# Expert outputs of an RWKV-5 and mixture-of-experts kernel: transposed by VectorE into pieces of 96 values, and one prefix product placed earlier

## The chip, the cores and the metric

The kernel runs on one core of a Trainium2 chip. The metric is the device time of one execution in microseconds. Before the change it is 455.46 us, the median of 9 runs that lie between 454.89 and 457.84 us. All profiles are of one execution on that core; times in them count from the first instruction of the span. Engines are TensorE (PE; its weight loads are PEld), VectorE (DVE), ScalarE (ACT), GpSimd (POOL) and SyncE (SP, which only issues DMAs here).

## The reference

Two blocks follow each other, everything in FP32.

The first is a recurrence over time (RWKV-5): 4 batches, 8 heads, 768 steps, a head of 48 values. Its outputs, taken as 3072 rows (tokens) of 384 values, enter the second block, a mixture of experts in two levels: 4 groups of 4 experts. Each token goes to one expert, and its result is scaled by two softmax weights:

```python
g_idx = np.argmax(x @ w_group, axis=1)
# within the chosen group g:
e_idx = np.argmax(xg @ w_expert[g], axis=1)
# for the tokens of expert (g, e):
h = np.maximum(xg[mask_e] @ w1[g, e], 0.0)     # 384 -> 1024
ye = h @ w2[g, e]                              # 1024 -> 384
out[tok_idx] = combined[:, None] * ye          # combined: product of the two gates
```

So each token is computed by one of 16 experts of 384 x 1024 and 1024 x 384 weights (3 MB together), and its row goes back to the place of the token.

## The kernel before

**First stage** (to about 155 us). 24 tiles of 128 tokens go through the recurrence in matrix form, in a loop of 29 steps in which each tile is at another point of its way (`turn`, `scores`, `values`, `back`, `rows_T`, `row_logits`). The order of the instructions of all engines is that of the program text here. `route` works out the choice of tokens in groups of two or four tiles, in five parts that the loop places at steps of its own: `choice` (arg-max, one-hot, exponential), `before` (L395: two products that count, for every token, how many tokens of its expert come ahead of it: the prefix product), `gate` (softmax weights), `place` (L417: the row number in the expert's region) and `rows` (L423: an indirect DMA by GpSimd that writes 128 rows of 384 values and two extra ones, the token's number and its gate, into `x_sorted`). `choice`, `before` and `gate` work in the PSUM bank `rb`, and the products of `before` go into a part of that bank, `pre`.

**Second stage.** `ITEMS` (L469) is a list of 17 pieces of work. Item 0 is the first 128 tokens of the fullest expert after four sixths of the tokens, which begins inside the first stage; item 1 is the rest of that expert, up to 256; items 2 to 16 are the other experts, in the order of their sizes. Each has a fixed number of slots (`SLOTS`, L20: 256, 240, 233, ... 178, 173). Tokens that don't fit would be done by a part at the end that these inputs don't need.

For an item:

- `load_rows` (L488, SP queue) reads the item's rows of `x_sorted` in blocks of 32 tokens, and the two extra values (`key`) with 128 tokens on partitions.
- `columns` (L508, VectorE) turns each 32 x 32 block, so that `xe` has the model dimension on partitions and tokens along the free dimension; then makes `ids` (token numbers) and `gates`, one token to a partition.
- `up` (L523, PE) computes two of eight blocks of 128 hidden values: the weights `w1` are the stationary operand (lhsT) and the tokens the moving one. ScalarE applies the ReLU into `hT`.
- `down` (L538, PE) computes one of three blocks of 128 output values, with 128 contiguous columns of `w2` as lhsT, over eight steps. ScalarE copies PSUM to `yo`, which has output values on partitions and tokens along the free dimension.
- `rows_out` (L571) calls `turn_out` (L555): TensorE transposes `yo` in blocks of 128 x 128 into PSUM (`pb`, L565), VectorE scales each row by its gate into `yt` (L567), and GpSimd scatters 128 rows of 384 values into `out` by an indirect DMA (L577). For 233 slots that is six transposes, two scalings and two DMAs.

Of item i, `rows_out` stands between `up(i + 1, 2)` and `up(i + 1, 4)`; for the last item a part of it stands inside its own last `down`. Weights have two places, the tiles `w1`/`w2` and the space of `kall`/`rall` of the first stage; the weights of expert e + 2 are issued on SP's queue when those of e have been read (L444, L449). In this stage only PE's order is written out; that of the other engines is made by the scheduler.

**The passage.** The last group of two tiles is routed while item 0 is computed. `before`, `gate`, `place` and the two `rows` of this group stand after `up(0, 4)` (L817 to L819). Item 1 can be loaded only when all rows are scattered: L821 follows on SP's queue and waits for the landing. Between stand `up(0, 6)`, `down(0, 0)` to `down(0, 2)` and `rows_out(0)` on PE.

Of the kernel before, what the change touches and what calls it, by code (L numbers as in the profile page):

```python
# [15 lines left out]
P = 128  # L16
# [18 lines left out]
def kernel(  # L35
# [312 lines left out]

    def route(pool, rb, xt, T, sums, number, group):

# [20 lines left out]
        place_f = part(1, "p (i a) -> p i a")  # L371
        pre = part(GE, "p (i e) -> p i e")
        mx, kx = tl([P, T, NA], "mx"), tl([P, T, NA], "kx")
# [108 lines left out]
    def room(i):  # L482
        return P if i == 0 else CAP

    def padded(n):
        return -(-n // BL) * BL

    def load_rows(i, expert, queue):  # L488
# [8 lines left out]
        n = room(i)  # L497
        xg, key = xgs[i] = tl([P, n // BL, KO, BL], "xg"), tl([P, n // P, ROW_EXTRA], "key")
        a, w, rows = ITEMS[i][1], padded(width(i)), regions[bass.ds(expert, 1)]
        for q in range(P // BL):  # L500
# [3 lines left out]
            )  # L504
        n = P * len(parts(i))
        queue.dma_start(out=key[:, 0 : n // P], in_=rows[:, a : a + n, DM:XW].rearrange("a (j p) w -> p (a j) w", p=P))

    def columns(i):  # L508
        xg, key = xgs.pop(i)
        w = padded(width(i))  # L510
        xe = xes[i] = item_tile(i, [P, KO, room(i)], "xe")
        for ko in range(KO):
            nc.vector.transpose(xe[:, ko, 0:w].rearrange("p (b t) -> p b t", t=BL), xg[:, 0 : w // BL, ko, :])  # L513
        ids = item_tile(i, [P, 2], "ids", U32, bufs=4)
        gates = item_tile(i, [P, 2], "gates", bufs=4)
        for j, n in enumerate(parts(i)):
            nc.vector.tensor_scalar(
                out=ids[0:n, j : j + 1], in0=key[0:n, j, ROW_ID : ROW_ID + 1], scalar1=float(N), scalar2=None, op0=OP.add
            )
            nc.vector.tensor_copy(gates[0:n, j : j + 1], key[0:n, j, ROW_GATE : ROW_GATE + 1])  # L520
        keys_of[i] = ids, gates

    def up(i, f):  # L523

# [4 lines left out]
        ph = bank([P, 2, w], "ph")  # L529
        for q in range(2):  # L530
            for ko in range(KO):
                nc.tensor.matmul(  # L532
                    ph[:, q, :], lhsT=w1[:, ko, P * (f + q) : P * (f + q + 1)], rhs=xe[:, ko, 0:w],
                    start=(ko == 0), stop=(ko == KO - 1), skip_group_check=True,
                )
        nc.scalar.activation(hTs[i][:, f : f + 2, 0:w], ph, AF.Relu)  # L536

    def down(i, d, beside=None):  # L538

        w = width(i)  # L540
        if d == 0:
            yo[i] = item_tile(i, [P, KO, room(i)], "yo")
        w2, hT = weights[ITEMS[i][0]][1], hTs[i]
        po = bank([P, w], "po")
        for fo in range(FO):
            if fo == FO // 2 and beside is not None:
                beside()
            nc.tensor.matmul(  # L548
                po, lhsT=w2[:, fo, P * d : P * (d + 1)], rhs=hT[:, fo, 0:w], start=(fo == 0), stop=(fo == FO - 1)
            )  # L550
# [4 lines left out]
    def turn_out(i, d0, d1):  # L555
# [6 lines left out]
        for j, n in enumerate(parts(i)):  # L562
            pb, yt = out_rows[i][j]
            for d in range(d0, d1):
                nc.tensor.transpose(pb[0:n, P * d : P * (d + 1)], yo[i][:, d, P * j : P * j + n], ident)  # L565
            cols = slice(P * d0, P * d1)
            nc.vector.tensor_scalar(  # L567
                out=yt[0:n, cols], in0=pb[0:n, cols], scalar1=gates[0:n, j : j + 1], scalar2=None, op0=OP.mult
            )

    def rows_out(i, d0=0):  # L571
# [138 lines left out]
    def routing(n):  # L710
# [5 lines left out]
            rpool, lgs.pop(n), xts[c][:, b0 : b + 1, :], T, cum[:, first : n + 2, :], tok[:, c, b0 : b + 1],  # L716
            "rows to places",
        )
# [97 lines left out]
    up(0, 2)  # L816
    up(0, 4)  # L817
    for _, part in todo.pop(NT + LAST):
        part()  # L819
# [24 lines left out]
    down(0, 2)  # L844
    rows_out(0)
    load_rows(2, second, nc.sync)
# [5 lines left out]
    with ExitStack() as moe:  # L852
        pools[1] = moe.enter_context(tc.tile_pool(name="moe", bufs=2, reuse_waits="tile"))
        with tc.manual_schedule(engines={mybir.EngineType.PE}):
            columns(1)
            for i in range(1, len(ITEMS)):
                up(i, 0)
                up(i, 2)
                if i > 1:
                    rows_out(i - 1)  # L860
                up(i, 4)
# [243 lines left out]
```

## Time and profile before

| | |
|---|---|
| median of 9 runs | 455.46 us (454.89 to 457.84) |
| the profiled execution | 454.51 us, span 452.7 us |
| TensorE busy | 430.9 us (95%) |
| its weight loads | 417.0 us (92%) |
| VectorE, ScalarE, GpSimd busy | 157.2, 138.9, 130.2 us |
| first product of the experts (L532), two groups | 72.9 and 68.4 us |
| second product (L548), two groups | 69.6 and 67.2 us |
| transposes of the outputs (L565) | 96, 13.7 us |
| row scalings (L567) | 34, 18.6 us |
| scatters into `out` (L577) | 32, 34.2 us |
| mean granted TensorE clock | 0.990 |
| DMA | 86.64 MB, 191 GB/s over the span |

Busy time of an engine is the time in which at least one of its instructions runs. TensorE's instructions overlap: a matmul of 196 columns lasts 0.33 us and starts 0.166 us after the one before. What one costs in a full stretch is therefore read from the starts in the timeline, and not from its length. In a group's line, "x" is the count, then come the busy time, the mean length in ns, and after the second bar the idle time of the engine ahead of these instructions with what ended it. The queue of SyncE is written SPq. An FP32 matmul appears as two records, a transpose as one.

### The profile page before, as it was taken

The numbers are of one execution on the slowest core, as the hardware profiler recorded it, in microseconds if no ns is written. First come the engines' busy times: TensorE is split into PE (matmuls) and PEld (weight loads), VectorE is DVE, ScalarE is ACT, GpSimd is POOL, SyncE is SP. The second block draws the span as 40 slices with busy tenths as digits, with TensorE's granted clock in tenths as the row PEclk, the third lists the DMA queues.
The fourth block names the chain that finished last, engine by engine and source line by source line (L and its number), as shares of the span: only waits on it lengthen the run. The fifth ranks groups of instructions, "written<-read, shape, count | busy, mean of one in ns | idle before, by whom it ended". The sixth has DMA issues, their size and how long they took to land. (4 is left out here: it accounts for less than half of the span.)

```text
span 452.7 us, 9343 instructions
## 1 busy us (share of the span) xinstructions
PE 430.9 (95%) x3553; PEld 417.0 (92%) x3553; DVE 157.2 (35%) x499; ACT 138.9 (31%) x418; POOL 130.2 (29%) x135
## 2 busy tenths in 40 slices
PE   7899999999999897999999999999999999999991
PEld 6699999899998797999999999999999999999991
DVE  6575777867785762011010110110110110111011
ACT  2885565456555321111111211211211121111110
POOL 7855536666653140001010210110210110221011
PEclk9999999999999989999999999999999999999997
DMA  9999999970117636999998887997997999999000
GB/s 171 240 244 223 251 268 228 186 141 36 38 37 177 206 109 157 266 266 197 278 260 203 207 236 163 256 244 168 252 251 172 264 243 213 233 246 245 30 25 27
DMA packets 126592, 86.64 MB, mean 191 GB/s; under 512 B 99532, under 2 KB 116084, under 8 KB 126540
## 3 DMA queue, kind: packets, MB, share of 16 engines
q1 hardware_dynamic: 115532, 69.19, 67.1%
q0 software_dynamic: 4624, 9.48, 6.4%
q10 hardware_dynamic: 6384, 7.31, 4.7%
q8 instruction: 29, 0.48, 0.5%
q14 instruction: 23, 0.19, 0.1%
HBM read 70.16 MB, written 16.12 MB: 191 GB/s over the span
## 5 line engine op out<-in xcount | busy, mean ns | idle before, releaser
L577 POOL DMA_INDIRECT out_dram<-yt,ids x32 | 34.2, 1068 | 242.7 <-DVE yt L567 238.1
L567 DVE TENSOR_SCALAR yt<-pb,gates 128x384 f32<-128x384 f32 (+18 forms) x34 | 18.6, 587 | 231.0 <-PE pb L565 231.0
L532 PE MATMUL ph<-xe,w 128*128 128x128 f32 (+7 forms) x432 | 72.9, 327 | 3.5 <-DVE xe L513 2.7
L532 PEld LDWEIGHTS ph<-xe,w 128*128 128x128 f32 x432 | 69.6, 196 | 4.2 <-issue 2.9
L548 PE MATMUL po<-hT,w 128*128 128x128 f32 (+7 forms) x432 | 69.6, 321 | 0.0
L536 ACT ACTIVATE hT<-ph 128x256 f32<-128x256 f32 (+15 forms) x68 | 33.6, 494 | 114.5 <-PE ph L532 99.0
L532 PE MATMUL ph<-xe,kall 128*128 128x240 f32 (+7 forms) x384 | 68.4, 335 | 0.2 <-DMA kall<-in_moe_w_dram 0.2
L548 PEld LDWEIGHTS po<-hT,w 128*128 128x128 f32 x432 | 68.0, 190 | 0.3
L548 PE MATMUL po<-hT,rall 128*128 128x240 f32 (+7 forms) x384 | 67.2, 334 | 0.0
L548 PEld LDWEIGHTS po<-hT,rall 128*128 128x128 f32 x384 | 65.3, 190 | 0.6
L532 PEld LDWEIGHTS ph<-xe,kall 128*128 128x128 f32 x384 | 64.9, 190 | 0.9 <-PE po L548 0.4
L551 ACT COPY yo<-po 128x128 f32<-128x128 f32 (+15 forms) x51 | 16.4, 321 | 115.1 <-PE po L548 115.1
L607 ACT ACTIVATE dv<-vt,du 128x48 f32<-128x48 f32 x192 | 45.9, 324 | 1.5 <-DVE du L601 1.5
L637 DVE TENSOR_TENSOR am<-pa,later 128x512 f32<-128x512 f32 x48 | 30.9, 686 | 6.8 <-PE pa L632 6.6
L425 POOL DMA_INDIRECT x_sorted<-xt,place_i x24 | 23.8, 990 | 27.0 <-DVE xe L513 13.8
L632 PE MATMUL pa<-rT,kT 48*128 48x128 f32 x384 | 28.7, 285 | 1.2 <-issue 0.7
L596 POOL TENSOR_TENSOR dg<-rall,kall 128x768 f32<-128x768 f32 x12 | 21.9, 1827 | 25.5 <-DVE du L601 25.5
L591 POOL TENSOR_TENSOR kh<-kall,T 128x768 f32<-128x768 f32 (+1 forms) x12 | 21.6, 1802 | 18.7 <-DMA kall<-in_k_dram 17.1
L632 PEld LDWEIGHTS pa<-rT,kT 48*128 48x128 f32 x384 | 23.9, 187 | 3.0 <-issue 1.1
L654 PE MATMUL py<-am,vt 128*64 128x128 f32 x384 | 26.5, 279 | 0.0
L622 ACT COPY kT<-pk 128x512 f32<-128x512 f32 x24 | 14.0, 584 | 34.0 <-PE pk L618 26.8
L654 PEld LDWEIGHTS py<-am,vt 128*64 128x64 f32 x384 | 20.7, 136 | 3.2 <-issue 0.5
(128 smaller groups left out, 439.6 us busy)
## 6 DMA issues: line engine op xcount, KB each, us to landing
w<-in_moe_w_dram SPq DMA_DIRECT2D x32, 384.0 KB
w<-in_moe_w_dram SPq DMA_DIRECT2D x8, 1536.0 KB
kall<-in_moe_w_dram SPq DMA_DIRECT2D x32, 384.0 KB
rall<-in_moe_w_dram SPq DMA_DIRECT2D x8, 1536.0 KB
x_sorted<-nothing ACTq DMA_DIRECT2D x4, 1544.0 KB
rall<-in_r_dram SPq DMA_DIRECT2D x12, 384.0 KB
vt<-in_v_dram SPq DMA_DIRECT2D x12, 384.0 KB
kall<-in_k_dram SPq DMA_DIRECT2D x10, 384.0 KB
```

The costliest lines, as they stand in the source:

```text
L425: ins = nc.gpsimd.indirect_dma_start(out=xs_dram, out_offset=bass.IndirectOffsetOnAxis(ap=place_i[:, i : i + 1], axis=0), in_=xt[:, i, :], ...
L532: nc.tensor.matmul(ph[:, q, :], lhsT=w1[:, ko, P * (f + q) : P * (f + q + 1)], rhs=xe[:, ko, 0:w], start=(ko == 0), stop=(ko == KO - 1), s ...
L536: nc.scalar.activation(hTs[i][:, f : f + 2, 0:w], ph, AF.Relu)
L548: nc.tensor.matmul(po, lhsT=w2[:, fo, P * d : P * (d + 1)], rhs=hT[:, fo, 0:w], start=(fo == 0), stop=(fo == FO - 1))
L567: nc.vector.tensor_scalar(out=yt[0:n, cols], in0=pb[0:n, cols], scalar1=gates[0:n, j : j + 1], scalar2=None, op0=OP.mult)
L577: ins = nc.gpsimd.indirect_dma_start(out=out, out_offset=bass.IndirectOffsetOnAxis(ap=ids[0:n, j : j + 1], axis=0), in_=yt[0:n], in_offset ...
L591: engine.tensor_mul(khs[g % (RING - 1)][:, a0:a1, :, 0:D], kts[g % RING][:, a0:a1], spread(T2[m], 1, a1 - a0))
L596: nc.gpsimd.tensor_mul(dg, rts[g % RING][:, :, :, 0:D], kts[g % RING])
L607: nc.scalar.mul(dv[:, h, :], vts[g % (RING + 1)][:, a, h, 0:D], dvs[g][:, a, h : h + 1])
L632: nc.tensor.matmul(pa[e][:, hc, :], lhsT=kT[rows, hc, :], rhs=rT[rows, hc, :], start=True, stop=True, skip_group_check=True,)
L637: nc.vector.tensor_mul(am[:, e], pa[e], spread(later, 1, HP))
L654: nc.tensor.matmul(py[DP * e : DP * (e + 1), hc, :], lhsT=vt[:, a, 2 * hc + e, :], rhs=am[:, e, hc, :], start=(c == 0), stop=True, skip_gr ...
```

## The change

1. For all items but the last, `rows_out` is replaced by `pieces_out`. VectorE turns `yo` in blocks of 32 x 32 (three instructions, one for each third of the output values), writing with a step of three values; one product scales by the gates; GpSimd scatters. A token's row is now spread over four partitions, one of each quarter, with 96 values in each, and so goes out as four pieces: one indirect DMA writes 128 pieces of 96 values, for 32 tokens.
2. For these pieces to be contiguous in the output, block d of `down` computes the output values d, d + 3, d + 6, ... instead of 128 neighbouring ones. The lhsT of `down` is therefore a view of `w2` with a step of three values, for all items, the last one too. The last item's `turn_out` undoes it by writing `yt` with that step.
3. `key` is loaded with 32 tokens on partitions; `ids` and `gates` hold each number four times, once for every quarter of the partitions, as numbers of pieces (eight small operations instead of four).
4. Where an item's slots are no multiple of 32, the rest of `yo` is filled with zeros.
5. `pieces_out(0)` stands in the second stage, after `columns(1)` in the text; the others stand where `rows_out` stood.
6. The last group's `before` runs inside `up(0, 4)`, between its two halves, and its `pre` has a PSUM bank of its own.

```diff
-    def route(pool, rb, xt, T, sums, number, group):
+    def route(pool, rb, xt, T, sums, number, group, apart=False):
...
-        pre = part(GE, "p (i e) -> p i e")
+        pre = bank([P, T, GE], "pre") if apart else part(GE, "p (i e) -> p i e")
...
-        xg, key = xgs[i] = tl([P, n // BL, KO, BL], "xg"), tl([P, n // P, ROW_EXTRA], "key")
+        xg, key = xgs[i] = tl([P, n // BL, KO, BL], "xg"), tl([P, n // BL, ROW_EXTRA], "key")
...
-        n = P * len(parts(i))
-        queue.dma_start(out=key[:, 0 : n // P], in_=rows[:, a : a + n, DM:XW].rearrange("a (j p) w -> p (a j) w", p=P))
+        p = P if is_last(i) else BL
+        n = -(-w // p) * p
+        queue.dma_start(out=key[0:p, 0 : n // p], in_=rows[:, a : a + n, DM:XW].rearrange("a (j p) w -> p (a j) w", p=p))
...
+            for q in range(P // BL):
+                part, b = slice(BL * q, BL * (q + 1)), w // BL
+                nc.vector.tensor_scalar(
+                    out=ids[part, 0:b], in0=key[0:BL, 0:b, ROW_ID], scalar1=float(P // BL),
+                    scalar2=float(N * (P // BL) + q), op0=OP.mult, op1=OP.add,
+                )
+                nc.vector.tensor_copy(gates[part, 0:b], key[0:BL, 0:b, ROW_GATE])
...
-    def up(i, f):
+    def up(i, f, beside=None):
...
         for q in range(2):
+            if q == 1 and beside is not None:
+                beside()
...
             yo[i] = item_tile(i, [P, KO, room(i)], "yo")
+            if w < padded(w):
+                nc.vector.memset(yo[i][:, :, w : padded(w)], 0.0)
...
-                po, lhsT=w2[:, fo, P * d : P * (d + 1)], rhs=hT[:, fo, 0:w], start=(fo == 0), stop=(fo == FO - 1)
+                po, lhsT=w2[:, fo].rearrange("p (c k) -> p k c", k=KO)[:, d], rhs=hT[:, fo, 0:w], start=(fo == 0), stop=(fo == FO - 1)
...
-                out=yt[0:n, cols], in0=pb[0:n, cols], scalar1=gates[0:n, j : j + 1], scalar2=None, op0=OP.mult
-            )
+                out=yt[0:n].rearrange("p (c k) -> p k c", k=KO)[:, d0:d1],
+                in0=pb[0:n, cols].rearrange("p (k c) -> p k c", c=P),
+                scalar1=gates[0:n, j : j + 1], scalar2=None, op0=OP.mult,
+            )
+
+    def pieces_out(i):
+
+        y, (ids, gates) = yo.pop(i), keys_of.pop(i)
+        w = padded(width(i))
+        b = w // BL
+        yr = item_tile(i, [P, room(i) // BL, BL, KO], "yr")
+        for d in range(KO):
+            nc.vector.transpose(yr[:, 0:b, :, d], y[:, d, 0:w].rearrange("p (b t) -> p b t", t=BL))
+        yp = item_tile(i, [P, room(i) // BL, KO * BL], "yp")
+        nc.vector.tensor_mul(
+            yp[:, 0:b], yr[:, 0:b].rearrange("p b d k -> p b (d k)"), spread(gates[:, 0:b], 2, KO * BL)
+        )
+        out_pieces = out.rearrange("n (q d) -> (n q) d", d=KO * BL)
+        for j in range(b):
+            ins = nc.gpsimd.indirect_dma_start(
+                out=out_pieces, out_offset=bass.IndirectOffsetOnAxis(ap=ids[:, j : j + 1], axis=0), in_=yp[:, j],
+                in_offset=None, bounds_check=N * (P // BL) - 1, oob_is_err=False,
+            )
...
-            "rows to places",
+            "rows to places", n == NT - 1,
...
-    up(0, 4)
-    for _, part in todo.pop(NT + LAST):
+    placing = [part for _, part in todo.pop(NT + LAST)]
+    up(0, 4, placing[0])
+    for part in placing[1:]:
         part()
...
-    rows_out(0)
     load_rows(2, second, nc.sync)
...
             columns(1)
+            pieces_out(0)
...
                 if i > 1:
-                    rows_out(i - 1)
+                    pieces_out(i - 1)
```

## The prediction

> **What bounds the kernel now.** I read the page's busy table first, then the groups by line, then the timeline of one middle item, then that of the passage into the expert stage, and last the DMA share in 2 us windows.
>
> The page's busy table and one of its groups (busy us, mean ns of one | idle before):
>
> ```profile
> PE 430.9 (95%) x3553; PEld 417.0 (92%) x3553; DVE 157.2 (35%) x499; ACT 138.9 (31%) x418; POOL 130.2 (29%) x135
> ...
> L577 POOL DMA_INDIRECT out_dram<-yt,ids x32 | 34.2, 1068 | 242.7 <-DVE yt L567 238.1
> ```
>
> TensorE is full, the others are a third full; what leaves PE shortens the run, if nothing else becomes late. Three groups by line:
>
> ```profile
> L565 PE MATMUL pb<-ident,yo 128*128 128x128 f32 (+15 forms) x96 | 13.7, 274 | 0.5 <-ACT yo L551 0.4
> L565 PEld LDWEIGHTS pb<-ident,yo 128*128 128x128 f32 (+15 forms) x96 | 11.3, 134 | 1.5 <-ACT yo L551 1.0
> L654 PEld LDWEIGHTS py<-am,vt 128*64 128x64 f32 x384 | 20.7, 136 | 3.2 <-issue 0.5
> ```
>
> L565 is what the change takes away: 96 transposes. Of L654 I use the length of a 64-column weight load. Next, the timeline inside the item with 196 tokens (start us, length us; x counts merged records; each FP32 product appears as two records):
>
> ```profile
> 331.69 4.14 PE L532 MATMUL ph<-xe,kall 128*128 128x196 f32 x24
> ...
> 335.67 0.82 PE L565 MATMUL pb<-ident,yo 128*128 128x128 f32 x6
> ...
> 336.33 4.15 PE L532 MATMUL ph<-xe,kall 128*128 128x196 f32 x24
> ...
> 340.31 8.12 PE L548 MATMUL po<-hT,rall 128*128 128x196 f32 x48
> ```
>
> No idle stands in brackets: products, six transposes and products again follow without a gap. From 335.67 to 336.33 the six transposes take 0.66 us, 0.110 each. 48 records of L548 take (8.12 - 0.33) / 47 = 0.166 each, the 0.33 being one record's own length; that is 0.847 ns per token.
>
> The passage into the expert stage, where item 0 (128 tokens) ends and item 1 waits for the sorted rows:
>
> ```profile
> 148.40 0.75 PEld L466 LDWEIGHTS rb<-gw,xT 128*128 128x128 f32 x6
> ...
> 159.84 4.55 PE L532 MATMUL ph<-xe,w 128*128 128x128 f32 x24
> ...
> 164.23 0.31 PE L396 MATMUL rb<-ohe,later 128*128 128x32 f32 x2
> ...
> 164.38 0.39 PE L400 MATMUL rb<-cum,ones 128*128 128x32 f32 x2
> ...
> 164.87 0.20 DVE L406 TENSOR_REDUCE rb<-ex 128x10 f32<-128x40 f32 x1 [1.32 <-ACT hT L536]
> ...
> 166.23 0.16 DVE L421 CAST place_i<-rb 128x2 uint32<-128x2 f32 x1
> ...
> 168.44 0.98 POOL L425 DMA_INDIRECT x_sorted<-xt,place_i  x1 [0.30 <-issue]
> ...
> 171.25 1.87 SPq L501 DMA_DIRECT2D xg<-x_sorted  x4
> ...
> 171.60 0.85 PE L565 MATMUL pb<-ident,yo 128*128 128x128 f32 x3
> ...
> 174.73 0.70 DVE L513 STREAM_TRANSPOSE xe<-xg 128x128 f32<-128x128 f32 x3 [1.62 <-DMA xg<-x_sorted]
> ...
> 175.19 5.60 PE L532 MATMUL ph<-xe,w 128*128 128x128 f32 x48 [2.73 <-DVE xe L513]
> ```
>
> Here PE stands still for 2.73 us at the end of a chain: prefix product, gate, place, scatter of the rows, their landing, the load of item 1's rows, their transposes. What shortens that chain shortens the run. The first line gives a bound on weight loads: six loads of 128 FP32 columns, whose products have 20 columns and so hide nothing, start (0.75 - 0.19) / 5 = 0.112 us apart.
>
> The DMA share (second number from the right; the rate in GB/s is last) through an item:
>
> ```profile
> 332.00:334.00 2.00, 2.00 (x14) 2.00 (x13) 0.00 (x0) 0.28 (x2) 0.00 (x0) 1.00 0.56 93
> ...
> 340.00:342.00 2.00, 2.00 (x14) 2.00 (x14) 0.00 (x0) 0.50 (x1) 0.22 (x1) 1.00 0.36 79
> ...
> 348.00:350.00 2.00, 2.00 (x14) 2.00 (x13) 0.00 (x0) 0.32 (x1) 0.00 (x0) 1.00 0.63 120
> ```
>
> The share falls each time just before the next weights are issued (340.5, 348.5), so a batch has landed by then, one item (some 16 us) before its first use. That slack is missing once, at the start of item 2:
>
> ```profile
> 186.36 5.10 PE L532 MATMUL ph<-xe,kall 128*128 128x240 f32 x24 [0.22 <-DMA kall<-in_moe_w_dram]
> ```
>
> **The change part by part.**
>
> *Transposes off PE.* Of the 96, the last item keeps 6. Item 0's 3 run at 171.60, in front of a wait that ends by another chain: worth nothing. The other 87 (3 of item 1, 6 each of items 2 to 15) lie between products: 87 x 0.110 = 9.5 us. By L565's busy time it would be 87 x 0.143 = 12.4, but that counts the pipeline's tail; start to start decides.
>
> *The second product reads w2 at a step of 3 values.* Every lhsT of L548 becomes columns d, d+3, d+6 ..., for the pieces to be whole. No operand of before has such a step, so the load of 128 columns is bounded from both sides: 0.112 us (contiguous, L466) to twice the columns' part. A 64-column load takes 136 ns and a 128-column one 190 (L548), so 128 columns cost 2 x 54 = 108 and the upper end is 0.220. Below 0.112 gains nothing, since the products set the pace there: 0.847 ns x tokens is 0.147 at 173 and 0.203 at 240. So a load up to 0.147 is hidden in all items but 0 and 1, where 128 tokens also need 0.112. I take no cost: L565 loads 128 columns in 140 ns, 50 less than L548, so the memory can hand over contiguous values about twice as fast as an FP32 product asks, and a step has that much to spare. At 0.220 the sum of 48 x (0.220 - pace) is 5.2 for item 1, 0.8 at 240 tokens, 2.6 at 196, 3.5 at 173: 40 us over items 1 to 16.
>
> [...]
>
> *VectorE instead.* Per item three transposes like L513 (0.36 each), one product of 128 x 768 (some 1.1, doubling L591's 0.56 for 384), eight small operations on 32 partitions in place of four (0.13 each) and a fill (0.3): about 3 us in items of 14 to 19, on an engine busy 2.2 of 20 there. Writing at a step of 3 may double the transposes: still hidden. Two places are tighter. In the changed order, item 0's transposes and product stand ahead of item 1's row transposes: they can start when yo is complete (172.07) and need 0.3 + 0.56, to 173.0, against rows landing at 173.7 or later. Item 1's first transpose stands ahead of item 2's row transposes: yo's first third is copied at 182.87, then 0.3 + 1.1 ends at 184.3; PE asks at 186.1. Both covered, by 0.7 and 1.8 us. The fill stands ahead of the ScalarE copy into yo, one item early.
>
> *GpSimd scatters.* 104 instead of 30: four in items 0 and 1, eight to six after. Their spacing is 1.28 (167.16 to 168.44), so 10.2 to 7.7 us per item: hidden, and the last item's two find the queue empty, since six end some 10 us into an item of 16. What would uncover it: a spacing over 2.2.
>
> *DMA.* The same bytes in four times the pieces. Nearest prices: queue 1's mean packet, 0.671 x 16 x 452.7 / 115,532 = 42 ns, and queue 0's, 0.064 x 16 x 452.7 / 4,624 = 100 ns. 104 x 128 pieces at 42 ns on 16 engines are 35 us in 250, 0.14 of share; the old rows were about 0.06 there. The share goes from 0.9 to about 1.02 with the shorter items, and 1.08 stood over 40 to 80 us without PE idling. Hidden by the 16 us of slack, except at item 2: item 0's four scatters now fall into that load. 512 pieces at 42 ns are 1.3 us against 0.8 before (128 at 100): I add 0.3, bounds 0 and 1.3. The key load keeps its place and count in SP's queue.
>
> [...]
>
> *Prefix product earlier.* It moves ahead of the second half of `up(0, 4)`, six records, and into a bank of its own, so that the gate no longer waits for it. Its inputs are there (cum at 163.44, PE reaches it at 163.65, 0.59 earlier). The gate then waits for the exponential alone (163.82): L406 starts at 163.9 instead of 164.87, the place at 165.3, and the scatters (kept up by nothing else: GpSimd is free from 163.8), the load and item 1 follow 0.96 earlier. ScalarE's copy of the token number moves behind `up(0, 4)`'s activation, to 165.3: not later than the place. That holds with PE as slow as here: 24 records in 4.55 us are 0.19 each, where 0.112 is the pace, and the clock of 160 to 164 us is 0.57. In executions without this, PE waits for cum anyway and only the bank gives, 0.3. Bounds 0 and 0.96; I take 0.7.
>
> *Tail.* The last item's row scaling writes at a step of 3: 0.30 each for two, 0 to 0.6 added; I take 0, by the same pieces' length today.
>
> Sum: -9.5 - 0.7 + 0.3 = -9.9. The profiled execution, 454.51 with a span of 452.7 and 1.8 around it, goes to 444.6; the median of the runs, 455.46, is 0.95 above it and goes to 445.5.
>
> **The rivals.**
>
> *Strided weight loads become the bound.* For it: PEld is 92% busy, hence close behind PE, and nothing shows such a load. Against: the factor of two between the loads of L565 and L548. A load of 0.165 costs 5.1 us over items 1 to 16 (450.6); 0.190 costs 18.2 (463.8); 0.220 costs 40 (486). It passes to slower at about 0.175, which is 1.56 of today's. Item 0 would then also end later and push its VectorE work in front of item 1.
>
> *GpSimd or VectorE becomes the bound.* The scatters of an item outlast it, yp's two buffers fill, and VectorE holds item rows back. Needs 2.2 us per scatter; the longest of L577 is 1.82. At 3 us, 104 take 312 in a stage of 262: 495.
>
> *The DMA is full and weights come late.* If each piece costs what queue 0's packet does now, 100 ns, pieces add 83 us of 250, share 1.2; at the 1.08 that was held the stage grows by some 28, less 9.9: about 473.
>
> *The prefix product does nothing,* since the wait for the rows ends by another link: 446.2, inside the forecast.
>
> **How the numbers follow.** Forecast, loads hidden: 0.70, its own range 443.6 to 447.5. Loads between 0.125 and 0.175, still faster: 0.09, up to 455. Loads above that: 0.12, slower. GpSimd, VectorE or DMA the bound: 0.07, slower. Within 0.2% (about 0.9 us, what a measurement of this kernel tells from no change): 0.02. So 0.79 faster, 0.19 slower. The range runs from 443.6 (445.0 with all bounds favourable, and 1.4 for the spread of runs and what L565's busy time may hold beyond the spacing) to 454.5, which takes in the middle case and leaves the slower ones out.
>
> **What would show it.** In the profile after: 6 L565-like transposes instead of 96, 104 scatters; PE's products back to back through the middle of each item; the second product's records at the same spacing as before (0.166 at 196 tokens, 0.147 at 173) says the step is free, one spacing for all narrow items says the load sets it. The wait before item 1 should end about 0.9 us earlier after the place, and that of item 2 on kall should stay under 0.6. Waits of PE for xe in later items would mean VectorE is late; waits on w, kall or rall, the DMA. The prediction is wrong first if a load at a step of 3 takes over 0.15 us.

## The result and the profile after

The changed kernel took 465.18 us, the median of 15 runs between 461.72 and 467.72, against 455.29 of the kernel before (46 runs, 454.33 to 457.84): a ratio of 1.0207, interval 1.0189 to 1.0224. It is slower by 9.9 us, where 9.9 us less were forecast. Single executions, of the kernel before too (up to 464.22 us), are some 6 to 10 us longer than the others of their kernel, and the ratios leave these out. One thing more has to be said at once: in two later measurements, on two chips, the same program took 453.16 us (0.9963, 0.9935 to 0.9991) and 452.85 us (0.9952, 0.9922 to 0.9982), while the kernel before had 454.3 to 455.8 in all of them. The profile of the first measurement is called "after" here; it took 462.97 us, with a span of 461.2.

The busy line of the page of after, and three groups by line (busy us, mean ns of one | idle before):

```profile
PE 437.4 (95%) x3463; PEld 423.1 (92%) x3463; DVE 187.2 (41%) x616; ACT 138.7 (30%) x418; POOL 198.8 (43%) x209
...
L605 POOL DMA_INDIRECT out_dram<-yp,ids x104 | 101.0, 971 | 177.7 <-DVE yo L560 133.8 <-issue 27.2 <-DVE xe L517 8.5
L566 PEld LDWEIGHTS po<-hT,w 128*128 128x128 f32 x432 | 77.7, 258 | 4.6 <-ACT hT L552 4.6
...
L583 PE MATMUL pb<-ident,yo 128*128 128x128 f32 (+1 forms) x6 | 1.0, 282 | 0.4 <-ACT yo L569 0.4
```

The transposes are gone as forecast (6 instead of 96) and GpSimd issues 104 scatters. But PE is busy 6.5 us longer, and a weight load of the second product lasts 258 ns instead of 190. The timeline of the item with 196 tokens in after (start, length, merged records):

```profile
336.47 8.12 PE L548 MATMUL ph<-xe,kall 128*128 128x196 f32 x48
344.43 8.56 PE L566 MATMUL po<-hT,rall 128*128 128x196 f32 x48
```

The first product is as before; the second takes 8.56 instead of 8.12 us. In the item with 128 tokens the records show the load itself, because there it is slower than the products, which at 0.847 ns per token would start 0.108 us apart. The passage into the expert stage in after:

```profile
164.59 0.31 PE L396 MATMUL pre<-ohe,later 128*128 128x32 f32 x2
...
165.61 0.16 DVE L421 CAST place_i<-rb 128x2 uint32<-128x2 f32 x1
...
167.19 8.62 PE L566 MATMUL po<-hT,w 128*128 128x128 f32 x48
...
170.71 1.85 SPq L504 DMA_DIRECT2D xg<-x_sorted  x4
...
175.84 0.27 ACT L569 COPY yo<-po 128x128 f32<-128x128 f32 x1 [2.56 <-PE po L566]
...
176.52 0.56 DVE L600 TENSOR_TENSOR yp<-yr,gates 128x384 f32<-128x384 f32 x1
177.00 0.69 DVE L517 STREAM_TRANSPOSE xe<-xg 128x128 f32<-128x128 f32 x3
...
177.35 7.25 PE L548 MATMUL ph<-xe,w 128*128 128x128 f32 x48 [1.55 <-DVE xe L517]
```

48 records in 8.62 us, one of them 0.339 long, start (8.62 - 0.339) / 47 = 0.176 us apart. Before, they took 5.60 us here (0.112) and 5.52 in item 1 (0.110). The place comes 0.62 us earlier than before and the rows are loaded 0.54 earlier; yet item 1 starts 2.16 later. Its transposes on VectorE now stand behind the product of item 0, and that behind the copy of the last third of `yo`, which starts 4.0 us later (175.84 for 171.80): 1.0 because the second product starts later, 3.0 because it is longer.

Then there is a thing that no step of the prediction had. The timeline of after in the item with 190 tokens:

```profile
377.99 0.97 POOL L605 DMA_INDIRECT out_dram<-yp,ids  x1 [0.30 <-issue]
...
378.41 2.25 PE L566 MATMUL po<-hT,rall 128*128 128x190 f32 x12
379.27 0.97 POOL L605 DMA_INDIRECT out_dram<-yp,ids  x1 [0.30 <-issue]
380.55 0.97 POOL L605 DMA_INDIRECT out_dram<-yp,ids  x1 [0.30 <-issue]
381.57 2.27 SPq L444 DMA_DIRECT2D kall<-in_moe_w_dram  x4
381.57 0.49 ACT L552 ACTIVATE hT<-ph 128x380 f32<-128x380 f32 x1 [3.85 <-remote]
...
382.11 6.61 PE L566 MATMUL po<-hT,rall 128*128 128x190 f32 x36 [1.46 <-ACT hT L552]
```

PE begins the second product at 378.41, so the last block of the first one is complete by about 378.6. ScalarE's activation and SyncE's weight load both wait for that, on the same semaphore of TensorE (103 in the trace), and both start at 381.57, 3.0 us later, in the same moment. PE runs out of activations and stands still for 1.46 us. TensorE's signal reached neither of them for 3 us. The same place in a later profile of the same program (run e13 below):

```profile
372.14 0.97 POOL L605 DMA_INDIRECT out_dram<-yp,ids  x1 [0.30 <-issue]
...
372.55 2.25 PE L566 MATMUL po<-hT,rall 128*128 128x190 f32 x12
372.75 1.86 SPq L444 DMA_DIRECT2D kall<-in_moe_w_dram  x4
372.75 0.49 ACT L552 ACTIVATE hT<-ph 128x380 f32<-128x380 f32 x1 [1.44 <-PE ph L548]
```

Here both start 0.20 us after PE begins the next product. In the list of waits of after such lateness makes these rows (us in total, times, longest; `remote` and `issue` say that the profile shows nothing that ended the wait); the profile of e13 has none of the three:

```profile
ACT hT L552 <- remote: 25.0, 7, 4.4
ACT hT L552 <- issue: 21.5, 11, 3.6
...
PE po L566 <- ACT hT L552: 5.8, 5, 1.5
```

I call these late signals from here on; how late is the time from the end of the product's last record to the start of the activation or copy that waits for it, elsewhere 0.04 to 0.1 us (0.38 at one place, the first activation of item 7, in most of the profiles, the one before among them). What follows is easiest to read from one table. It is worked out from the timelines: the time from the first product of an item to that of the next, for item 16 to PE's last record; "end" is what lies behind. All in us.

| profile | first stage | item 0 | items 1, 2 | items 3 to 16 | end | span |
|---|---|---|---|---|---|---|
| before | 155.24 | 19.95 | 31.02 | 237.28 | 9.21 | 452.7 |
| after | 155.20 | 22.15 | 34.91 | 242.82 | 6.12 | 461.2 |
| e13, the same program as after | 153.84 | 22.16 | 34.90 | 234.34 | 6.26 | 451.5 |
| e17, the same program as after | 153.73 | 22.16 | 33.27 | 234.34 | 6.10 | 449.6 |
| e1, before + step of three | 154.17 | 21.29 | 35.21 | 243.57 | 9.26 | 463.5 |
| e14, after without the step | 154.00 | 19.36 | 34.33 | 228.08 | 6.23 | 442.0 |
| e16, shifted copies | 154.06 | 19.15 | 31.26 | 228.08 | 6.15 | 438.7 |
| e10, scatters later | 155.68 | 22.16 | 34.90 | 234.90 | 6.36 | 454.0 |
| e9, step in odd items | 155.41 | 19.37 | 33.27 | 242.70 | 6.25 | 457.0 |
| e11, quarter of the bytes | 155.36 | 23.43 | 33.42 | 246.26 | 6.33 | 464.8 |
| e12, plain DMAs | 157.09 | 23.78 | 33.28 | 234.34 | 6.30 | 454.8 |
| e7, scatters that write nothing | 153.83 | 23.53 | 33.28 | 234.34 | 6.32 | 451.3 |

Where no signal is late, items 3 to 16 take the same time to 0.01 us in four profiles of the stepped program: 234.34. After has 8.48 us more there, and this is what the late signals cost in these items in its profile, which is of one of the shorter executions (462.97 of 461.72 to 467.72).

### The profile page after: what moved, and what is told of

The parts are those of the page before. It is cut to its first block, busy times and chain, and to the rows that moved or that the text cites. A ratio compares the mean times of both kernels' runs of the same rounds, so it can differ in the third digit from the quotient of the medians.

```text
span 461.2 us, 9430 instructions
## 1 busy us (share of the span) xinstructions
PE 437.4 (95%) x3463; PEld 423.1 (92%) x3463; DVE 187.2 (41%) x616; ACT 138.7 (30%) x418; POOL 198.8 (43%) x209
## 5 line engine op out<-in xcount | busy, mean ns | idle before, releaser
L605 POOL DMA_INDIRECT out_dram<-yp,ids x104 | 101.0, 971 | 177.7 <-DVE yo L560 133.8
L598 DVE STREAM_TRANSPOSE yr<-yo 128x224 f32<-128x224 f32 (+3 forms) x48 | 22.2, 463 | 204.0 <-ACT yo L569 203.9
L566 PE MATMUL po<-hT,w 128*128 128x128 f32 (+7 forms) x432 | 79.3, 343 | 3.8 <-ACT hT L552 3.8
L566 PEld LDWEIGHTS po<-hT,w 128*128 128x128 f32 x432 | 77.7, 258 | 4.6 <-ACT hT L552 4.6
L566 PE MATMUL po<-hT,rall 128*128 128x240 f32 (+7 forms) x384 | 72.0, 346 | 2.4 <-ACT hT L552 2.0
L548 PEld LDWEIGHTS ph<-xe,w 128*128 128x128 f32 x432 | 71.5, 201 | 3.0 <-DVE xe L517 1.7
L566 PEld LDWEIGHTS po<-hT,rall 128*128 128x128 f32 x384 | 70.2, 257 | 3.5 <-ACT hT L552 2.5
L548 PE MATMUL ph<-xe,kall 128*128 128x240 f32 (+7 forms) x384 | 67.0, 334 | 0.0
```

The source lines that it names most:

```text
L548: nc.tensor.matmul(ph[:, q, :], lhsT=w1[:, ko, P * (f + q) : P * (f + q + 1)], rhs=xe[:, ko, 0:w], start=(ko == 0), stop=(ko == KO - 1), s ...
L566: nc.tensor.matmul(po, lhsT=w2[:, fo].rearrange("p (c k) -> p k c", k=KO)[:, d], rhs=hT[:, fo, 0:w], start=(fo == 0), stop=(fo == FO - 1))
L598: nc.vector.transpose(yr[:, 0:b, :, d], y[:, d, 0:w].rearrange("p (b t) -> p b t", t=BL))
L605: ins = nc.gpsimd.indirect_dma_start(out=out_pieces, out_offset=bass.IndirectOffsetOnAxis(ap=ids[:, j : j + 1], axis=0), in_=yp[:, j], in_ ...
```

## The experiments

The kernel before ran beside each group of experiments, and each ratio is to that. Runs e1 to e4 were on one chip, e5 to e8 on a second, e9 to e12 on a third, e13 to e16 on a fourth, e17 and e18 on a fifth. The first theory was: the step of three in the weights is the loss. The rivals: the many scatters, or the passage.

**One part at a time.** e1 is the kernel before with the step alone, e2 with the prefix product alone:

```diff
-                po, lhsT=w2[:, fo, P * d : P * (d + 1)], rhs=hT[:, fo, 0:w], ...
+                po, lhsT=w2[:, fo].rearrange("p (c k) -> p k c", k=KO)[:, d], rhs=hT[:, fo, 0:w], ...
```

> The kernel before with one edit: the second product reads w2 at a step of three values, and the row scaling undoes the order. TensorE's transposes, whole-row scatters and the old place of the prefix product stay. Theory A (the step alone makes a weight load take 0.174 to 0.176 us): the second product's records start 0.174 to 0.176 apart in every item of 206 tokens or fewer, and items 1 to 16 lose 9 to 10 us, item 0 up to 3 more; 465 us, and the activations of the last quarter of the first product start on time (0.04 us after their product), since nothing crowds GpSimd. Theory B (the step also makes completion signals of TensorE late): the same spacing, and besides activations that start 1 to 3 us after their product, with TensorE idle in the second product; 468 to 472 us.

> The kernel before with only the prefix product moved into up(0, 4) and given its own bank. As predicted, item 1 starts 0.3 to 0.96 us earlier: 454.4 to 455.1 us. In the changed kernel the rows of item 1 were asked for 0.54 us earlier than before (170.71 against 171.25), which gives 454.8. If the wait for the rows ends by another link, 455.3.

Measured: e1 464.29 us, 1.0223 (1.0191 to 1.0254), so the step alone costs 9.8 us; no signal is late in its profile. e2 453.85 us, 0.9988 (0.9965 to 1.0010): not distinguishable from nothing.

e3 is the changed kernel with the same line undone, e4 with one scatter for an item instead of four to eight:

```diff
-                po, lhsT=w2[:, fo].rearrange("p (c k) -> p k c", k=KO)[:, d], rhs=hT[:, fo, 0:w], ...
+                po, lhsT=w2[:, fo, P * d : P * (d + 1)], rhs=hT[:, fo, 0:w], ...
```
```diff
-        for j in range(b):
+        for j in range(1):
```

> The changed kernel with the second product reading 128 neighbouring columns of w2 again; nothing else. The values inside a token's row then come out in another order, so its output is not the reference's; the work is the same. Theory A and B of the step: spacing back to 0.847 ns per token (0.166 at 196), no late activations, no idle of TensorE in the second product; the prediction's own sum, 445.5 us (444.5 to 446.5). Theory C (the 104 scatters make TensorE's signals late, whatever the step): activations 1 to 3 us late stay, TensorE idles some 6 us, and the time is 450 to 452.

> The changed kernel with only the first of each item's piece scatters (16 of 104); the rest of the output is not written. Theory C (scatters make the signals late): the late activations and the 6 us of idle go, 458 to 460 us. Theory B (the step makes them late): they stay, 464 to 466 us.

Measured: e3 442.57 us, 0.9752 (0.9732 to 0.9772). So everything but the step gives 11.9 us (454.46 to 442.57). e4 454.80 us, 1.0002 (0.9985 to 1.0019). At this point 9.8 and -11.9 came near to e4 (+0.3), but not to the 465 of the changed kernel: some 12 us stood open, and I took them for something that steps and scatters do to each other. These four runs could not tell: no signal is late in any of their profiles, on this chip.

**Step of two, and pieces without a step.** e8 is the kernel before with a step of two values:

```diff
-                po, lhsT=w2[:, fo, P * d : P * (d + 1)], ...
+                po, lhsT=w2[:, fo, 0 : 2 * P].rearrange("p (c k) -> p k c", k=2)[:, 0], ...
```

> The kernel before, with the second product's weights read at a step of two values instead of neighbouring ones (every block takes the same even columns, so the outputs are those of other columns). [...] If any step costs: one spacing for all narrow items, between 0.147 and 0.176 us; at 0.176 the time is that of the step of three, 464.

Measured: 453.33 us in the profiled run, a span of 451.6 (the only other run took 462.09, so there is no ratio). The second product of item 1 (128 tokens) in e8:

```profile
179.67 5.82 PE L548 MATMUL po<-hT,w 128*128 128x128 f32 x48
```

That is (5.82 - 0.339) / 47 = 0.117 us for a load, against 0.110 contiguous and 0.176 at a step of three; a load lasts 196, 190 and 258 ns. In all wider items the products hide 0.117, and items 3 to 16 take 237.3 us as before. So it is not that there is a step: one of two adds 0.007 us to a load, one of three 0.066. What makes the difference between them is not shown; no other step was run.

e5 makes the same pieces with contiguous weights. ScalarE's three copies out of PSUM become twelve of 32 partitions, each of which moves its values to the right quarter:

```diff
+            for a in range(P // BL):
+                q, k = (P // BL * d + a) // KO, (P // BL * d + a) % KO
+                nc.scalar.copy(yo[i][BL * q : BL * (q + 1), k, 0:w], po[BL * a : BL * (a + 1)])
```

e6 also issues the second expert's weights ahead of item 1's rows:

```diff
     up(0, 6)
+    weights[1] = load_expert(second, 1)
     load_rows(1, first, nc.sync)
```

> Compute the same pieces without a step in the weights: the second product reads 128 neighbouring columns of w2 again, and ScalarE's copy out of PSUM, three instructions of 128 partitions before, becomes twelve of 32 partitions, each moving its 32 values to the quarter of yo where a contiguous piece wants them. If the stepped weight load alone (by its own pace and by what it does to the scatters) is what made the change slower: about 443.5 us, ratio 0.975, as with the contiguous columns and the values out of order; second product's records of narrow items at 0.147 to 0.166 us again, no late activations. If the nine more ScalarE copies per item (at the 0.23 us that a narrow ScalarE copy takes, some 2 us more per item on an engine that is 30% busy) hold up the next item's activations: more than 446.

> As the run before, and the second expert's weights are issued before item 1's rows instead of after item 2's rows. If PE's wait of 2.65 us for kall at the start of item 2 (seen with contiguous columns) is an issue that came too late: that wait is gone and the time is 1.5 to 2.7 us below the run before, about 441.5, ratio 0.971. If the weights only compete with the rows of item 1 for the DMA engines: item 1 starts later by what item 2 gains, no difference.

Measured: e5 442.99 us, 0.9736 (0.9687 to 0.9784); e6 444.97 us, 0.9782 (0.9735 to 0.9830). Two groups of e5:

```profile
L574 ACT COPY yo<-po 32x128 f32<-32x128 f32 (+14 forms) x192 | 59.9, 312 | 80.0 <-PE po L566 77.9
...
L566 PEld LDWEIGHTS po<-hT,w 128*128 128x128 f32 x432 | 68.0, 190 | 0.3
```

A copy of 32 partitions takes as long as one of 128 (314 ns in e16 and 322 in after, both at 196 tokens), so ScalarE works 44 us more in the whole run and is busy 42%. PE loses nothing by it: items 3 to 16 take 228.08 us in e16, with these copies, and in e14, without them. e6 missed its aim: it is no faster than e5, and their intervals overlap. The start of item 1 in e6 and in e5:

```profile
177.67 8.05 PE L548 MATMUL ph<-xe,w 128*128 128x128 f32 x48 [4.63 <-DVE xe L517]
```
```profile
172.84 5.62 PE L548 MATMUL ph<-xe,w 128*128 128x128 f32 x48 [2.66 <-DVE xe L517]
```

Item 2 does not wait for its weights (0.26 us in e5), but item 1's rows stand behind them and its wait grows from 2.66 to 4.63 us. In this one profile the rows are the more urgent of the two.

**Nothing written.** e7 raises the piece numbers beyond the output:

```diff
-                    scalar2=float(N * (P // BL) + q), op0=OP.mult, op1=OP.add,
+                    scalar2=float(N * (P // BL) + q + 2**20), op0=OP.mult, op1=OP.add,
```

> The changed kernel with all the piece numbers raised beyond the end of the output, so that the 102 scatters of items 0 to 15 are issued by GpSimd as before but write nothing (the pieces of these items are left out of the output). Stepped weight loads stay. If the late activations come from the pieces' traffic on the DMA engines: they vanish, and the time is that of the run with few scatters, about 454.8, ratio 1.00. If they come from GpSimd's own work of issuing (reading indices, writing descriptors): the time stays near 465, ratio 1.02, with PE's idle times of 0.2 to 1.5 us in the second product.

Measured: 452.36 us, 0.9955 (0.9932 to 0.9979), no late signal (the scatters are 104). I read it then as the pieces' traffic being the cause. The repeats below take that reading away: the whole changed kernel has 453 us and the same 234.34 on two other chips. What e7 does show is that without late signals it makes no difference to PE whether the pieces are written.

**What the late signals go with.** The next four ran on a chip where they did occur. e9 has the step in odd items only; e10 holds the transposes of item i - 1 back until the last activation of item i; e11 writes 24 of the 96 values of each piece; e12 issues plain DMAs, without indices, to consecutive places of a scratch tensor:

```diff
+                po, lhsT=w2[:, fo].rearrange("p (c k) -> p k c", k=KO)[:, d] if i % 2 else w2[:, fo, P * d : P * (d + 1)], ...
```
```diff
+        if i > 0:
+            nc.vector.tensor_copy(yr[0:1, 0, 0:1, 0], hTs[i + 1][0:1, FO - 1, 0:1])
         for d in range(KO):
```
```diff
-                out=out_pieces, out_offset=bass.IndirectOffsetOnAxis(ap=ids[:, j : j + 1], axis=0), in_=yp[:, j],
+                out=out_pieces, out_offset=bass.IndirectOffsetOnAxis(ap=ids[:, j : j + 1], axis=0), in_=yp[:, j, 0 : KO * BL // 4],
```
```diff
-            ins = nc.gpsimd.indirect_dma_start(
+            ins = nc.gpsimd.dma_start(out=pieces_dram[at : at + P], in_=yp[:, j])
```

> The changed kernel, but only the items of odd number read w2 at a step of three values; those of even number read neighbouring columns (their values come out in another order). If an activation is late only where stepped loads run beside the item's own scatters: late activations in the odd items alone, none over 0.2 us in the even ones; about 454 us. If the stepped loads of the item before leave something behind: late activations in the even items. If the lateness comes of the stage being long as a whole: in both kinds.

> The changed kernel with one small VectorE copy that makes the transposes of item i - 1 wait for the last activation of item i, so that the scatters run beside the second product of item i and the first products of item i + 1, instead of beside the first products of item i. If any matmul's signal is late while scatters run and stepped loads are queued: the late ones are now the copies of yo in the second product, and the time stays near 465. If it takes the change from the first to the second product during the scatters: the lateness is gone, and the time is near 455.

> The changed kernel, but each piece of 96 values is cut to its first 24: the same number of pieces, a quarter of the bytes (the other values are not written). If the late signals go by the number of pieces: the same lateness and near 465. If they go by bytes: a quarter of it, near 457.

> The changed kernel, but GpSimd issues each set of 128 pieces as a plain DMA to consecutive places of a scratch tensor in DRAM, with no indices (the outputs of items 0 to 15 stay unwritten). If the pieces' bytes leaving SBUF while stepped loads run are the cause: lateness as in the changed kernel, near 465. If it takes the scattered places or the indices: no lateness, near 453 to 455.

| run | us | ratio to before | late signals |
|---|---|---|---|
| e9 | 458.73 (7 runs, 454.39 to 462.54) | 1.0042 (0.9989 to 1.0096) | in odd and even items, up to 4.3 us |
| e10 | 455.51 | 0.9984 (0.9964 to 1.0003) | up to 3.1 us, but PE hardly waits for them |
| e11 | 465.25 (2 runs) | 1.0198 (1.0115 to 1.0282) | as in after, up to 3.7 us late |
| e12 | 454.83 | 0.9973 (0.9954 to 0.9991) | none |

In e9 the item with 190 tokens is an even one, whose weights are read contiguously:

```profile
378.90 0.97 POOL L605 DMA_INDIRECT out_dram<-yp,ids  x1 [0.31 <-issue]
379.93 2.24 SPq L444 DMA_DIRECT2D kall<-in_moe_w_dram  x4
379.94 0.49 ACT L552 ACTIVATE hT<-ph 128x380 f32<-128x380 f32 x1 [3.85 <-remote]
...
380.48 2.84 PE L566 MATMUL po<-hT,rall 128*128 128x190 f32 x16 [1.63 <-issue]
```

So it doesn't take a stepped load running at the time: the last activation is 3.02 us late here and 3.00 in after. In e11 a quarter of the bytes makes the signals no less late, so it is not the bytes. In e12 the same number of DMAs of the same pieces, without indices, has no late signal. Three things differ in it: there are no indices, the places are consecutive, and GpSimd is done with the six of an item in 3.18 us instead of 7.36. Which of them counts is not shown. In e10 the scatters run beside the second product and the beginning of the next item. The signals are late there too, as these lines of e10 show, but they are such as PE can do without for a while (the copy of the last third, the first activation of four); only item 16 is longer, by 0.56 us, and items 3 to 16 take 234.90:

```profile
368.53 0.97 POOL L607 DMA_INDIRECT out_dram<-yp,ids  x1 [0.30 <-issue]
...
369.50 0.32 ACT L569 COPY yo<-po 128x193 f32<-128x193 f32 x1 [4.75 <-PE ph L548]
...
371.11 0.87 ACT L552 ACTIVATE hT<-ph 128x380 f32<-128x380 f32 x2 [1.29 <-PE ph L548]
```

The late copy starts where a scatter ends (368.53 + 0.97), and so does the late activation of after (380.55 + 0.97 for 381.57). In after and e9 to e11, all 28 signals that were over 2 us late for a free ScalarE came when the last of an item's scatters had ended, or up to 1.84 us behind it; none of these came in the middle of them. Of the less late ones some did: the activation of after at 243.56, 1.85 us late, starts where a scatter ends, 1.27 us before the end of the last.

**The program or the chip.** e13 and e17 are the changed kernel, e14 is e3, e16 and e18 are e5, all once more. e15 has the step in item 8 alone:

```diff
+                po, lhsT=w2[:, fo].rearrange("p (c k) -> p k c", k=KO)[:, d] if i == 8 else w2[:, fo, P * d : P * (d + 1)], ...
```

> The changed kernel once more, beside the variants with contiguous columns on the same chip. If the late signals belong to the program: 465, ratio 1.02, with late activations in items 2 to 16. If they belong to a chip: 455 without them on this one, or 465 here and the contiguous variant near 452 instead of 443.

> The pieces with contiguous columns (values in another order) once more. If the late signals need the stepped loads: none, ratio 0.975, about 443. If the scatters alone make them, on some chips: late activations here too, about 452.

> The changed kernel with the step of three in item 8 alone, the other items with contiguous columns (their values in another order). If the late signals need stepped loads running at the time: only in item 8 or 9, about 444. If a stepped load anywhere in the program changes all items: late activations in all of them, about 453.

> ScalarE's shifted copies with contiguous columns once more, on the chip of the changed kernel. If the steps are the cause of all the loss: 443, ratio 0.974, no late activations. If the scatters make signals late on some chips whatever the weights: about 452 here.

> The changed kernel on one more chip. If this chip is of the kind of the first measurement: about 465 and late activations beside the scatters; if of the kind of the run before: about 453, none late.

> ScalarE's shifted copies with contiguous columns, on the same chip. Where the changed kernel has late signals: late activations here too and about 452 if indexed scatters of small pieces are enough, none and 443 if the stepped loads are needed as well. Where the changed kernel has none: 442 to 443.

| run | us | ratio to before |
|---|---|---|
| e13, changed kernel | 453.16 | 0.9963 (0.9935 to 0.9991) |
| e14, without the step | 441.61 | 0.9696 (0.9638 to 0.9754) |
| e15, step in item 8 | 441.87 | 0.9713 (0.9658 to 0.9767) |
| e16, shifted copies | 441.87 | 0.9723 (0.9676 to 0.9769) |
| e17, changed kernel | 452.85 | 0.9952 (0.9922 to 0.9982) |
| e18, shifted copies | 443.24 | 0.9741 (0.9704 to 0.9779) |

No signal is late in any of the six, and the changed kernel takes 453 us instead of 465 (the kernel before 454.3 and 454.4 instead of 455.3). So they don't belong to the program alone: a chip, or something else in which the measurements differed, decides with it. On one chip the step costs 453.16 - 441.61 = 11.6 us; e15's single stepped item is longer by 0.20 us (16.60 for 16.40), and no other.

**The kernel before has them too.** It has no step, and its expert stage no burst of scatters; but in its first stage four scatters of whole rows follow each other, from 136.95 us on. Here is that place in its profile, and below it in that of e8, which differs from the kernel before only in its second products (a product, the last scatter of the four, and ScalarE's copy of the product):

```profile
140.35 1.09 PE L654 MATMUL py<-am,vt 128*64 128x128 f32 x16
140.78 0.97 POOL L425 DMA_INDIRECT x_sorted<-xt,place_i  x1 [0.30 <-issue]
...
143.02 0.59 ACT L659 COPY yT<-py 128x512 f32<-128x512 f32 x1 [2.03 <-PE py L654]
```
```profile
140.08 1.09 PE L654 MATMUL py<-am,vt 128*64 128x128 f32 x16
140.33 0.97 POOL L425 DMA_INDIRECT x_sorted<-xt,place_i  x1 [0.30 <-issue]
...
141.27 0.58 ACT L659 COPY yT<-py 128x512 f32<-128x512 f32 x1 [0.56 <-PE py L654]
```

The product ends at 141.44 and the copy starts 1.58 us later; in e8 it is 0.10. All twenty profiles divide in this way: 1.57 to 1.62 us in before, after and e9 to e12, and 0.10 in the other fourteen. So neither a step nor small pieces are needed, and every profile tells of which kind its measurement was. That e12 is of the late kind, too, makes its expert stage without a late signal a fair test. The first stage is longer where the signals are late: 155.2 to 157.1 us, for 153.7 to 154.2. The kernel before loses about 1 us by this; the changed one has 106 scatters behind its first stage instead of 32, most of them in bursts of six to eight.

**What stays open.** How much the pieces without a step (e3, e5) lose where signals are late: they ran only where none was. Since the kernel before has late signals without a step, some loss is to be expected there. Also what makes the difference between the measurements (the chip, or where the tensors lay, or another circumstance), and how a signal of TensorE becomes late beside indexed scatters. The runs show with what it goes (indexed scatters in a burst, of pieces or of rows; not their bytes, not plain DMAs, not a step), not the mechanism. And whether the first measurement was on the chip of e9 to e12 is not on record.

The version with shifted copies beats both kernels wherever it ran: it is 2.6 to 2.8% below the kernel before on three chips, and 9.6 to 11.3 us below the changed kernel on the two where both ran. The reservation is the one just made.

## Why the prediction was wrong

*The step that failed* is "The second product reads w2 at a step of 3 values ... I take no cost". The load at that step takes 0.175 to 0.176 us, between my bounds of 0.112 and 0.220. The argument for the lower end was that a transpose's weights load 50 ns faster than a product's, so that the memory had speed to spare. This said something about how fast contiguous values come and nothing about values at a step, which take 0.117 us at two and 0.176 at three. The load is somewhat above the middle of the bounds, 0.166. The term measures +6.3 us in items 3 to 16 (e14 to e13), +3.0 in item 1 (8.53 us for 5.52 in e1) and some +2.8 in item 0 (19.36 to 22.16), about 12 us for a term of zero. I had named 0.175 as the point from which the change loses, and left item 0 out of it. With the gains below it comes out 1.1 to 1.6 us ahead on two chips, so near the point indeed.

*What no step had* is the late signals. Where the kernel was first measured the change costs 9.9 us, and on the two chips without them it gains 1.1 and 1.6: they make some 11 us. The rival "GpSimd or VectorE becomes the bound" was about the scatters' spacing, and that stayed at 1.28 us as taken. In the expert stage no row of before could show the effect, because there the scatters are two for an item. A row of its first stage did, the copy at 143.02 us above, but the prediction took no row from that place. The slower cases had 0.19 together, 0.12 of it for the stepped load.

*Transposes off PE,* -9.5: right. Items 3 to 16 lose 0.66 each (237.28 to 228.08 is 9.20), item 2 loses 0.33 (19.77 in e8 to 19.44 in e17), together 9.53.

*VectorE instead:* hidden in items 2 to 16, as taken. The cover of 0.7 us in the passage was worked out with item 0's second product as it was. When this grew by 3 us the cover was gone, and item 0's transposes and product hold up item 1's. In e5 the rows are ready 3.44 us after they are asked for (169.03 to 172.47); by that they would be in after at about 174.15, and their transposes start at 177.00. One wrong term removed the ground of another.

*GpSimd's and the DMA's time:* hidden where no signal is late, as the 234.34 with and without writing show. The first load of item 2 was a term of 0.3 with bounds of 0 and 1.3. It was exceeded in two profiles, where PE waited 2.65 (e3) and 2.15 us (e14), and met in two others with 0.26 (e5) and 0.77 (e16). The line of e14:

```profile
186.50 7.79 PE L548 MATMUL ph<-xe,kall 128*128 128x240 f32 x29 [2.15 <-DMA kall<-in_moe_w_dram]
```

*Prefix product earlier,* -0.7: the place comes 0.62 earlier in after, but what this is worth is not shown. Item 0 takes 19.36 us in e14 and 20.51 in e3, which have the early product and no step, and 18.76 in e8, which has the late one. Alone it can't be told from nothing (e2): there item 0 takes 18.97 us instead of 19.95, and items 1 and 2 take 32.19 instead of 31.02.

*Tail,* 0: wrong in the other direction. The end is 3 us shorter in every kernel with all the pieces. The last lines of before and of after:

```profile
445.35 0.91 POOL L577 DMA_INDIRECT out_dram<-yt,ids  x1 [0.30 <-POOLq L879]
```
```profile
456.95 0.91 POOL L618 DMA_INDIRECT out_dram<-yt,ids  x1 [0.30 <-POOLq L921]
```

From the end of the last scatter to the end of the span it is 452.7 - 446.3 = 6.4 us before and 461.2 - 457.9 = 3.3 after. These 3 us are most of the way from the -9.9 of the sum to the -12.65 that the change gives without the step (454.26 to 441.61). The terms as measured, -9.5, -3, +12 and +11, add up to some +10.5, for the +9.9 of the first measurement.

## What to carry to other kernels

Before a layout is bought with a step in a stationary FP32 operand, measure the load at that very step: 128 columns took 0.110 us here contiguous, 0.117 at a step of two and 0.176 at a step of three. It counts where the product is shorter than the load: up to 202 tokens here (a record each 0.171 us before, 0.175 in after), and no more at 206 (0.174 in both). Let an engine with idle time make the layout instead, as ScalarE did here with 44 us of extra copies by which PE lost nothing (228.08 us for items 3 to 16 in e16 and e14). And when the parts measured alone don't add up to the whole, run the whole again beside them on the same chip before looking for an interaction, and look for the odd wait in the kernel before, in all its stages.

## What the hardware showed that was not expected

- Signals of TensorE came up to 4.3 us late (e9), at two waiting engines in the same moment, while GpSimd issued bursts of indexed scatters, of small pieces and, in the kernel before, of whole rows (1.58 us); in six of twenty profiles only.
- The end of the span, behind the last scatter, is 6.4 us with 32 scatters of whole rows and 3.3 us with 104 of pieces and two of rows. With 18 scatters in all (e4) it is 5.1, and with the pieces by plain DMAs (e12) 3.5. Most of it is one DRAIN of GpSimd, of 4.72, 2.17, 3.58 and 2.29 us in these four. Why is open.
- The clock after a wait of PE differs without a visible reason. After the same 1.55 us of waiting the granted clock was 0.56 and 0.59 in the next 4 us of e13, and 1.00 in e17; this makes item 1 1.6 us longer in e13 (15.45 for 13.83). The line of e13 (us of PE, weight loads, VectorE, ScalarE, GpSimd, then clock, DMA share, GB/s):

```profile
176.00:178.00 2.00, 2.00 (x10) 2.00 (x11) 1.52 (x11) 0.00 (x0) 1.70 (x2) 0.56 0.83 207
```
